# Gated linear attention and a maxout MoE: an earlier MoE 0 and 1, ScalarE's order in units 2 and 3, and a last output in column halves

## The chip, the cores and the metric

The kernel runs on one core of one Trainium2 chip. The metric is device time in microseconds, the median of several executions. A profiled execution also gives a trace of every engine. Its "span" runs from the first to the last instruction and is some 1.7 us shorter than the device time of the same run. TensorE is PE in the profile, VectorE DVE, ScalarE ACT, GpSimd POOL and SyncE, which issues nearly all transfers, SP.

## The reference

```python
state = zeros((B, H, D, D))                 # B, H, S, D = 4, 8, 768, 48
for t in range(S):
    state = alpha[:, :, t, :, None] * state + einsum('bhd,bhe->bhde', k[:, :, t], v[:, :, t])
    y[:, :, t] = einsum('bhd,bhde->bhe', q[:, :, t], state)
x = y.transpose(0, 2, 1, 3).reshape(B * S, H * D)     # 3072 x 384
g = maximum(x @ w1, x @ w2)                           # 384 x 1024 weights
return g @ w_out                                      # 1024 x 384
```

## The kernel before

The work is cut into 12 units of 256 tokens. Unit u goes through attention: a logarithm of alpha, prefix sums by products with masks, exponentials, scaled q and k, transposes ("turn"), scores and a running state. Then it goes through the MoE. Because max(h1, h2) = relu(h1 - h2) + h2, the hidden part is relu(x(w1 - w2)) and the output is that times wo, plus x(w2 wo). The product w2 wo is summed once, by `wmul`, and `wsub` makes w1 - w2. The MoE of unit u-1 runs inside the iteration of unit u, and units 0 and 1 are written out ahead of the loop. PSUM is the memory, in banks, that TensorE's products are written to; in this program a bank is used again once another engine has read the result out of it. A "hidden product" below is one call of `hid`, a group of six matmuls:

```python
def hid(u, f2, on_act=None):       # 6 products of 256 columns, then a Relu that frees one of two PSUM banks "m"
    ...
def outx(u, n): ...                # op = x * (w2 wo): 3 products of 384 columns
def outg(u, n): ...                # op += g * wo: 8 products, copy to SBUF, output DMA
def outp(u, n): outx(u, n); outg(u, n)

# ... ahead of the loop
wmul(0); wcast(1); wsub(0)
pmm(1, 1); pmask(1, 1)
wmul(1)
wout()
load(3)
hid(0, 0, True)
wsub(1)
hid(0, 1, True)
wsub(2)
dummies(2)                         # warm-up products, their result is never used
hid(0, 2, True)
wsub(3)
dummies(2)
vcast(1)
hid(0, 3, True)
load(4)
ln(2)
outp(0, 0)
...
for f2 in range(4):
    hid(1, f2)                     # MoE 1 ahead of the loop
ln(3)
load(5)
for u in range(2, NU):
    if u + 4 < NU: load(u + 4)
    kvmm(u, 0); pmm(u, 0); ...
    if u > 2: hid(u - 1, 0); hid(u - 1, 1); sumd(u + 1); hid(u - 1, 2)
    else:     outp(1, 0); sumd(u + 1)
    ...
outp(NU - 1, 0)
outp(NU - 1, 1)
```

A load of one unit is alpha, k, q, v, in this order, on SyncE's queue.

Names in the profile lines: af is alpha as loaded and lg its logarithm; cs the prefix sums and their exponentials; qn and kn the scaled q and k, tp and qk their turn; kv, tm and sb the running state; ya and xn the output of attention, xp and xt its turn ("x turn"); hp a hidden product and gT its Relu; op and outs an output; wq and w2o the product w2 wo; w the weights w1 - w2.

## Time and profile before

| | before |
|---|---|
| device time, median (range) | 148.25 us (148.0 to 148.4) |
| span of the profiled run | 147.0 us |
| hidden products of MoE 0, 1, 2 start at | 27.20, 39.55, 51.10 us |
| one unit of the loop | 9.58 to 9.77 us |
| last hidden products; end of the last product; end | 136.80; 143.60; 147.0 us |

The prediction reads the busy line and the chain. The stretch that the change rebuilds looks like this on PE's timeline (start, busy time, engine, line, operation, output from inputs, count, and in brackets the idle time before with its releaser):

```profile
25.24 2.12 PE L461 MATMUL wq<-wo,w2T 128*128 128x384 f16 x12
27.20 1.47 PE L410 MATMUL hp<-xt,w 128*128 128x256 f16 x12
28.70 0.59 PE L482 MATMUL warm<-wz 128*128 128x512 f16 x2
29.35 0.81 PE L410 MATMUL hp<-xt,w 128*128 128x256 f16 x6
...
39.55 2.97 PE L410 MATMUL hp<-xt,w 128*128 128x256 f16 x24 [0.61 <-DVE xt L399]
```

The second half of w2 wo comes first (25.24). Then warm-up products stand between the hidden products, and both use the two banks "m": the third hidden product starts at 29.35, just after the second Relu ends (29.30). Weights are not what the last two wait for: VectorE's last subtraction ends at 29.23, and the fourth product starts at 30.66. MoE 1 is a block of 24 matmuls by itself, behind an idle PE.

### The profile page before, as it was taken

What the parts mean: (1) busy time and instruction counts of PE and PEld (TensorE: products, weight loads), DVE (VectorE), ACT (ScalarE), POOL (GpSimd) and SP (SyncE); (2) the same over time, 40 slices, a digit from 0 to 9 for tenths busy, and PEclk for the clock granted to TensorE, in tenths of its full rate; (3) what the DMA queues carried; (4) which work ended last, traced back from release to release, by engine and by line L of the source; (5) the groups of instructions that cost most, each with busy time, mean ns of one, the idle gap of its engine ahead of it and who ended that gap; (6) DMA issues with size and microseconds to landing.
All of it is one profiled execution on the core that took longest, in us unless ns stands there. A gap on an engine that the chain in (4) does not pass through costs nothing.

```text
span 147.0 us, 4239 instructions
## 1 busy us (share of the span) xinstructions
PE 136.3 (93%) x1681; PEld 97.7 (66%) x1681; DVE 87.4 (59%) x180; ACT 97.2 (66%) x199; POOL 56.5 (38%) x111
## 2 busy tenths in 40 slices
PE   6749978999899999999999999999999999998990
PEld 2325655666776787767877877677777777775750
DVE  6046988904648876757767867566675756670010
ACT  3467452777576878688687886886879768654511
POOL 7491262055405438154181381541913617310000
PEclk9995999999999999999999999999999999999999
DMA  4999999969989897797999987999979991020202
GB/s 108 269 371 306 310 367 342 225 121 215 183 177 207 137 304 116 145 239 130 234 229 157 311 133 167 286 156 281 194 155 294 173 365 43 0 107 4 107 12 95
DMA packets 76339, 28.58 MB, mean 194 GB/s; under 512 B 71712, under 2 KB 74528, under 8 KB 76320
## 3 DMA queue, kind: packets, MB, share of 16 engines
q1 hardware_dynamic: 76320, 28.32, 83.4%
q8 instruction: 13, 0.21, 0.6%
q14 instruction: 6, 0.05, 0.1%
HBM read 23.59 MB, written 4.72 MB: 193 GB/s over the span
## 4 chain that ended last, share of the span: by engine, by line
PE 86%; ACT 4%; DVE 4%; DMA 3%; issue 1%
PE hp L410 23%; PE op L436 21%; PE op L429 8%; PE tp L296 7%; PE pp L345 5%; PE cs L237 4%; PE wq L461 3%; PE ya L381 3%; PE warm L482 3%; DMA af<-in_alpha_dram 3%; PE xp L397 3%; PE kv L318 2%; DVE qk L303 2%; PE cs L223 2%; PE ya L369 1%; ACT cs L252 1%
## 5 line engine op out<-in xcount | busy, mean ns | idle before, releaser
L410 PE MATMUL hp<-xt,w 128*128 128x256 f16 x288 | 37.2, 273 | 0.8 <-DVE xt L399 0.6
L415 ACT ACTIVATE gT<-hp 128x512 f16<-128x512 f32 x46 | 27.4, 596 | 14.4 <-PE hp L410 13.7
L351 DVE TENSOR_TENSOR pt<-pp,um 128x512 f16<-128x512 f32 x48 | 30.9, 686 | 9.3 <-PE pp L345 8.8
L436 PE MATMUL op<-wo,gT 128*128 128x384 f16 x192 | 35.1, 326 | 0.0
L285 POOL TENSOR_TENSOR kn<-kf,Em 128x384 f16<-128x384 f32 x24 | 23.4, 997 | 23.7 <-ACT Em L247 23.7
L410 PEld LDWEIGHTS <-w 128*128 128x128 f16 x288 | 26.1, 97 | 6.1 <-issue 2.2
L436 PEld LDWEIGHTS <-gT 128*128 128x128 f16 x192 | 18.4, 98 | 11.3
L277 POOL TENSOR_TENSOR sb<-tm,dd 128x192 f16<-128x192 f32 x20 | 10.1, 506 | 38.5 <-DVE tm L331 17.2
L439 ACT COPY outs<-op 128x384 f32<-128x384 f32 x24 | 11.5, 478 | 17.1 <-PE op L436 16.9
L289 DVE TENSOR_TENSOR qn<-qf,cs 128x384 f16<-128x384 f32 x24 | 12.3, 550 | 12.3 <-ACT de L257 11.6
L331 DVE TENSOR_TENSOR tm<-kv,sb 64x192 f32<-64x192 f32 x32 | 11.3, 353 | 9.1 <-PE kv L318 6.9
L429 PE MATMUL op<-w2o,xt 128*128 128x384 f16 x72 | 15.6, 326 | 0.0
L303 DVE COPY qk<-tp 128x1024 f16<-128x1024 f16 x20 | 12.9, 686 | 4.3 <-PE tp L296 4.3
L205 POOL CAST v<-vf 64x384 f16<-64x384 f32 x24 | 12.0, 501 | 6.4 <-DMA vf<-in_v_dram 5.6
L247 ACT ACTIVATE Em<-cs 128x384 f32<-128x384 f32 x24 | 11.6, 485 | 4.1 <-PE cs L237 4.1
L207 ACT CAST v<-vf 64x384 f16<-64x384 f32 x24 | 12.2, 510 | 1.4 <-DMA vf<-in_v_dram 0.9
L482 PE MATMUL warm<-wz 128*128 128x512 f16 x33 | 11.3, 452 | 1.3 <-DVE halves L149 1.3
L193 ACT ACTIVATE lg<-af 128x768 f16<-128x768 f32 x12 | 10.1, 843 | 3.2 <-DMA af<-in_alpha_dram 3.0
L252 ACT ACTIVATE cs<-cs 128x384 f32<-128x384 f32 x24 | 11.8, 493 | 0.0
L296 PE MATMUL tp<-ident,kn 128*128 128x128 f16 x96 | 9.3, 218 | 2.0 <-DVE qn L289 2.0
L345 PE MATMUL pp<-qk 48*128 48x128 f16 x192 | 9.8, 221 | 0.8 <-DVE qk L301 0.8
L388 ACT CAST xn<-ya 128x384 f16<-128x384 f32 x24 | 10.4, 491 | 0.1
(60 smaller groups left out, 152.7 us busy)
## 6 DMA issues: line engine op xcount, KB each, us to landing
af<-in_alpha_dram SPq DMA_DIRECT2D x12, 384.0 KB, 6.0
vf<-in_v_dram SPq DMA_DIRECT2D x12, 384.0 KB, 4.9
out_dram<-outs SPq DMA_DIRECT2D x11, 384.0 KB, 4.6
kf<-in_k_dram SPq DMA_DIRECT2D x40, 96.0 KB, 4.6
qf<-in_q_dram SPq DMA_DIRECT2D x40, 96.0 KB, 4.1
w2f<-in_moe_w_dram SPq DMA_DIRECT2D x3, 512.0 KB, 6.0
wof<-in_moe_w_out_dram SPq DMA_DIRECT2D x2, 768.0 KB, 7.6
w1f<-in_moe_w_dram SPq DMA_DIRECT2D x4, 384.0 KB, 9.6
```

Of the source, the lines that this page charges most:

```text
L252: nc.scalar.activation(out=X["csv"][cc], in_=X["csv"][cc], func=ACTF.Exp)
L285: nc.gpsimd.tensor_mul(out=X["kn"][cc][:, :, 0:D], in0=part(u, "kf", cc), in1=X["Em"][cc])
L289: nc.vector.tensor_mul(out=X["qn"][cc][:, :, 0:D], in0=part(u, "qf", cc), in1=X["csv"][cc])
L296: nc.tensor.transpose(tp[:, n, j, :], pair(src, j), ident)
L303: nc.vector.tensor_copy(out=X["qk"][:, cc], in_=tp.rearrange("p n h t -> p (n h) t"))
L345: nc.tensor.matmul(pa[a][:, j, :], lhsT=qk[r, 1, j, :], rhs=qk[r, 0, j, :], start=True, stop=True)
L351: nc.vector.tensor_mul(out=pt[:, a], in0=X["pa", cc][a], in1=um.unsqueeze(1).to_broadcast([128, HP, C]))
L410: nc.tensor.matmul(hp[:, n, :], lhsT=w12[:, ds, f * 128 : (f + 1) * 128], rhs=X["xt"][:, ds].rearrange("p n t -> p (n t)"), start=(ds == 0 ...
L415: nc.scalar.activation(out=gT[:, 2 * f2 : 2 * f2 + 2, :], in_=hp, func=ACTF.Relu)
L429: nc.tensor.matmul(op, lhsT=X["xt"][:, ds, n, :], rhs=w2o[:, ds, :], start=(ds == 0), stop=False)
L436: nc.tensor.matmul(op, lhsT=X["gT"][:, f, n * C : (n + 1) * C], rhs=wo16[:, f, :], start=False, stop=(f == NF - 1))
L482: nc.tensor.matmul(warm, lhsT=wz[:, 0:128], rhs=wz, start=True, stop=True)
```

## The change

The intent is to put the second half of w2 wo into the gaps between the hidden products of MoE 0, to take MoE 1 into the loop, to let ScalarE take the logarithm and the v casts of units 2 and 3 ahead of output copies, and to make the last copy and transfer half as large. The cut below leaves out some moves ahead of MoE 0 (`wcast(0)`, warm-up products and the second turn of unit 1), and that the sums of w2 wo move from the banks "m", which the hidden products between them now need, to g0 and g1.

```diff
 def turn(u, cc):
-    tp = new(f"g{cc}", ...)
+    tp = new(f"g{cc if u else 2 + cc}", ...)     # PSUM banks of unit 0's turns
...
+def outlast(u, n):
+    for e in range(2):                           # column halves of the last output
+        c = slice(e * DM // 2, (e + 1) * DM // 2)
+        op = new("m", [128, DM // 2], FP32, 2, "oq")
+        ...
+        if e == 0: scalar.copy(...);        scalar.dma_start(...)
+        else:      vector.tensor_copy(...); sync.dma_start(...)
...
-    pmm(1, 0)
-    pmask(1, 0)
     wmul(0)
     wcast(1)
     wsub(0)
-    pmm(1, 1)
-    pmask(1, 1)
-    wmul(1)
-    wout()
+    pmm(1, 0)
+    wmul(1, (0,))
     load(3)
     hid(0, 0, True)
     wsub(1)
+    wmul(1, (1,))
     hid(0, 1, True)
     wsub(2)
-    dummies(2)
+    wmul(1, (2,))
     hid(0, 2, True)
     wsub(3)
-    dummies(2)
+    pmask(1, 0)
+    wout()
+    dummies(1)
+    hid(0, 3, True)
     vcast(1)
-    hid(0, 3, True)
     load(4)
+    pmm(1, 1)
+    pmask(1, 1)
     ln(2)
     outp(0, 0)
...
-    outp(0, 1)
+    outx(0, 1)
+    outg(0, 1, (0, 1, 2, 3))
...
     vcast(2)
-    for f2 in range(4):
-        hid(1, f2)
+    outg(0, 1, (4, 5, 6, 7))
     ln(3)
...                                               # in the loop, every u, also u = 2:
+        hid(u - 1, 0)
+        hid(u - 1, 1)
...
-        xturn(u)
         if nxt:
+            xturn(u)
             vcast(u + 1)
-        if u + 2 < NU:
-            ln(u + 2)
-        if u > 2:
-            outg(u - 1, 1)
+            if u + 2 < NU:
+                ln(u + 2)
+            outg(u - 1, 1)
+        else:
+            outg(u - 1, 1, (0, 1, 2, 3))
+            xturn(u)
+            outg(u - 1, 1, (4, 5, 6, 7))
...
-    outp(NU - 1, 1)
+    outlast(NU - 1, 1)
```

More of the change, by code (lines that the diff above doesn't have):

```diff
@@ L292, in turn @@
         X = st[u]
-        tp = new(f"g{cc}", [128, 2, HP, C], FP16, 1, "tp")
+        tp = new(f"g{cc if u else 2 + cc}", [128, 2, HP, C], FP16, 1, "tp")
         for n, src in ((1, X["kn"][cc]), (0, X["qn"][cc])):
@@ L429, in outx, with outg @@
             nc.tensor.matmul(op, lhsT=X["xt"][:, ds, n, :], rhs=w2o[:, ds, :], start=(ds == 0), stop=False)
-    def outg(u, n):
+    def outg(u, n, fs=tuple(range(NF))):
         X = st[u]
-        d, b = divmod(u, B)
         op = X["op"]
-        for f in range(NF):
+        for f in fs:
             nc.tensor.matmul(
@@ L438, in outg, with dst @@
             )
-        nc.scalar.copy(out=X["outs"][:, n, :], in_=op)
-        t0 = b * S + d * 2 * C
-        dst = out[t0 : t0 + 2 * C, :].rearrange("(p j) d -> p j d", j=2)
-        if u == NU - 1:
-            nc.sync.dma_start(out=dst[:, n], in_=X["outs"][:, n])
-        elif n == 1:
-            nc.sync.dma_start(out=dst, in_=X["outs"])
+        if fs[-1] == NF - 1:
+            nc.scalar.copy(out=X["outs"][:, n, :], in_=op)
+            if u == NU - 1:
+                nc.sync.dma_start(out=dst(u)[:, n], in_=X["outs"][:, n])
+            elif n == 1:
+                nc.sync.dma_start(out=dst(u), in_=X["outs"])
+    def dst(u):
+        d, b = divmod(u, B)
+        t0 = b * S + d * 2 * C
+        return out[t0 : t0 + 2 * C, :].rearrange("(p j) d -> p j d", j=2)
+    def outlast(u, n):
+        X = st[u]
+        for e in range(2):
+            c = slice(e * DM // 2, (e + 1) * DM // 2)
+            op = new("m", [128, DM // 2], FP32, 2, "oq")
+            for ds in range(ND):
+                nc.tensor.matmul(op, lhsT=X["xt"][:, ds, n, :], rhs=w2o[:, ds, c], start=(ds == 0), stop=False)
+            for f in range(NF):
+                nc.tensor.matmul(
+                    op, lhsT=X["gT"][:, f, n * C : (n + 1) * C], rhs=wo16[:, f, c], start=False, stop=(f == NF - 1)
+                )
+            if e == 0:
+                nc.scalar.copy(out=X["outs"][:, n, c], in_=op)
+                nc.scalar.dma_start(out=dst(u)[:, n, c], in_=X["outs"][:, n, c])
+            else:
+                nc.vector.tensor_copy(out=X["outs"][:, n, c], in_=op)
+                nc.sync.dma_start(out=dst(u)[:, n, c], in_=X["outs"][:, n, c])
     def wturn(ds):
@@ L453, with wmul @@
     wqs = []
-    def wmul(n):
-        if n == 0:
-            wqs.extend([new("m", [128, DM], FP32, 2, "wq") for _ in range(2)] + [new("g3", [128, DM], FP32, 1, "wq")])
-        for ds in range(ND):
+    def wmul(n, dss=(0, 1, 2)):
+        if not wqs:
+            wqs.extend(new(f"g{i}", [128, DM], FP32, 1, "wq") for i in (0, 1, 3))
+        for ds in dss:
             for f in range(4 * n, 4 * n + 4):
@@ L529 @@
     xturn(0)
+    wcast(0)
+    dummies(2)
     turn(1, 0)
+    turn(1, 1)
     dummies(2)
-    turn(1, 1)
-    wcast(0)
-    pmm(1, 0)
-    pmask(1, 0)
     wmul(0)
@@ L573 @@
     turn(2, 1)
-    dummies(1)
     xturn(1)
-    dummies(1)
     vcast(2)
-    for f2 in range(4):
-        hid(1, f2)
+    outg(0, 1, (4, 5, 6, 7))
     ln(3)
@@ L594 @@
             kvmm(u, 1)
-        if u > 2:
-            hid(u - 1, 0)
-            hid(u - 1, 1)
-            if nxt:
-                sumd(u + 1)
-            hid(u - 1, 2)
-        else:
-            outp(1, 0)
+        hid(u - 1, 0)
+        hid(u - 1, 1)
+        if nxt:
             sumd(u + 1)
+        hid(u - 1, 2)
         if nxt:
@@ L613 @@
         pmask(u, 1)
-        if u > 2:
-            hid(u - 1, 3, True)
+        hid(u - 1, 3, True)
         if nxt:
@@ L622 @@
             state(u + 1, 0)
-        outp(u - 1, 0 if u > 2 else 1)
+        outp(u - 1, 0)
         yin(u)
@@ L627 @@
             turn(u + 1, 1)
-        if u > 2:
-            outx(u - 1, 1)
-        xturn(u)
+        outx(u - 1, 1)
         if nxt:
+            xturn(u)
             vcast(u + 1)
-        if u + 2 < NU:
-            ln(u + 2)
-        if u > 2:
+            if u + 2 < NU:
+                ln(u + 2)
             outg(u - 1, 1)
+        else:
+            outg(u - 1, 1, (0, 1, 2, 3))
+            xturn(u)
+            outg(u - 1, 1, (4, 5, 6, 7))
     for f2 in range(4):
```

## The prediction

> **What bounds the kernel now.** I first read the busy line and the slices of the page, to see where TensorE is not full.
>
> ```profile
> PE 136.3 (93%) x1681; PEld 97.7 (66%) x1681; DVE 87.4 (59%) x180; ACT 97.2 (66%) x199; POOL 56.5 (38%) x111
> ...
> PE   6749978999899999999999999999999999998990
> ...
> DMA  4999999969989897797999987999979991020202
> ```
>
> From about 40 to 133 us TensorE (PE) is full: windows of 10 us between 60 and 120 us have 10.00 us of PE busy. A unit of the loop takes 9.66 us (hidden products start at 51.10, and at 60.76 one unit later). A gain can only come from the first 43 us, from the end, or from work taken away. The DMA row says that the transfers are almost as full as PE.
>
> Next, the chain of work that ended last, from 20 us on:
>
> ```profile
> 20.86 0.43 PE warm L482 x2
> ...
> 21.77 0.70 DVE qk L301
> ...
> 28.70 0.61 PE warm L482 x2
> ...
> 37.75 1.29 DVE qk L303 x2
> 39.03 0.47 DVE xt L399
> ```
>
> Idle products ("warm") and waits on VectorE copies stand on the path. Adding the chain's useful PE pieces from 20.4 us (turn of unit 1) to 50.9 us (unit 3 enters the loop) gives 24.9 us (the largest: w2·wo 4.1, hidden products 5.2, output products 7.2) of 30.5, so 5.6 us are idle or warm-up: that is the most this stretch can give.
>
> Third, the timeline of the end:
>
> ```profile
> 134.23 0.87 ACT L388 CAST xn<-ya 128x384 f16<-128x384 f32 x2
> ...
> 135.16 0.51 PE L397 MATMUL xp<-ident,xn 128*128 128x128 f16 x6 [0.45 <-ACT xn L388]
> ...
> 135.50 1.46 PE L436 MATMUL op<-wo,gT 128*128 128x384 f16 x8
> 135.70 0.56 DVE L399 COPY xt<-xp 128x768 f16<-128x768 f16 x1 [3.31 <-PE xp L397]
> ...
> 143.64 0.48 ACT L439 COPY outs<-op 128x384 f32<-128x384 f32 x1 [1.31 <-PE op L436]
> ```
>
> PE waits for the xn casts with a ready product (outg of the unit before) behind them. After the last product the end is copy 0.48, DMA 1.85 (issue 144.15, landing 146.00) and closing 1.0 us.
>
> Last, whether the loads can follow an earlier PE. For each unit I set the landing of its loads against the instruction that uses them. Slack of alpha before its logarithm: unit 3 3.55, unit 4 2.56, unit 5 0.85, unit 6 1.47, unit 7 2.12 us, then 2 and more. The tightest use:
>
> ```profile
> 59.11 0.84 ACT L193 ACTIVATE lg<-af 128x768 f16<-128x768 f32 x1
> 60.19 0.48 ACT L439 COPY outs<-op 128x384 f32<-128x384 f32 x1 [0.24 <-PE op L436]
> ```
>
> Alpha of unit 5 was issued at 51.03 and took 7.23 us, so it landed at 58.26.
>
> **What the Trainium skill says.** "TensorE: Matmul & The Clock Gate", section "Wait — 56ns, not 53.3ns?": warm matmuls start every N/2.4 GHz plus about 2.5 ns; 384 columns give 162.5 ns, and the trace agrees (eight in 1.30 us). So 192 columns are estimated at 82.5 ns, and halving the columns of the last output costs PE nothing. "ScalarE: Activation LUTs", section "What ACT_TABLE_LOAD costs": an instruction with immediates takes 186 ns plus 0.833 ns an element; 384 give 506, measured 478. From these I estimate 0.32 us for 192. "DMA: Bandwidth & Descriptors", section "Specifications", wants at least 512 B for line rate; here 71712 of 76339 packets are smaller, which agrees with engines some 90% busy at a mean of 194 GB/s. The same page, "Issuing engines are not separate DMA queues": issuing from another engine saves only issue time, so the new ScalarE issue of the last output gets no bandwidth of its own; no run shows this yet.
>
> **The change, part by part.** The order of the built program keeps the source's order on each engine; the DMA queue's order is the same in both. Its waits are on earlier DMAs and on uses four units back, never on recent compute, so landings stay where they are. I replay the new order with durations from the trace.
>
> 1. Units 0 and 1, w2·wo, MoE 0. Before, from 27.36 to 31.47 the four hidden products take 4.11 us for 24 x 0.109 = 2.62. Now the second half of w2·wo (12 x 0.163) lies between them, while VectorE makes w1-w2. The w1 quarters land at 23.90, 25.03, 26.16, 27.34 and each subtraction takes 0.95, so they are ready at 24.9, 26.0, 27.15, 28.3. PE reaches the four hidden products at 25.0, 26.3, 27.6 and, behind one warm product and its drain (0.43), 28.7: none waits. The masks of unit 1 now follow the four subtractions (28.3 to 29.5), so its second score product waits 0.2; the three w2o copies on ScalarE end at 30.25 and hold the third output product 0.06. The output of MoE 0 ends at 31.75 instead of 33.19: gain 1.44.
> 2. Unit 2. ScalarE has v of unit 1 until 31.7 and the logarithm until 32.46 (before 33.21), so the sums gain only 0.75 at their start and 1.0 at their end, where the second output product gains 0.9. The exponentials end at 35.14, the first qn at 35.7; PE, with only half of that output product, arrives at 35.0 and waits 0.7. Turns end at 36.7, the x turn and the rest of the output product at 37.66. v of unit 2 lands at 37.21 and its casts hold the kv products to 37.8 and 38.34. The hidden products of MoE 1 start at 38.51 inside a normal iteration. Without stalls those of MoE 2 start 9.66 later, at 48.17; before 51.10. Gain 2.9.
> 3. In that iteration alpha of unit 3 (landing 38.97) makes the logarithm end at 39.85, so the first Relu is late and the third hidden product waits 0.4; q of unit 3 lands at 44.81, its second turn waits 0.2. MoE 2 starts at 48.8. Gain 2.3.
> 4. Alpha of unit 5 cannot land before 58.26. The logarithm then ends at 59.1 and the output copy behind it, in ScalarE's order, at 59.55. The second hidden product of MoE 3 needs that copy's bank and would be due at 59.1: it waits 0.45. Before it started at 61.42, now at 59.58. **Gain 1.84**, and everything afterwards keeps it: alpha of unit 6 is 0.4 late, inside the 0.9 that the copy has free; the rest has slack of 2 us.
> 5. The end. The half output product (0.65) now fills the wait for xn; but the x turn stays at 135.2 on the old clock, and the xt copy ends at 136.3, where the last hidden product starts instead of at 136.80: 0.46. The chain of Relus behind it makes 0.62 of it by the last output. The halves: the last matmul ends 0.6 earlier, VectorE's copy of 192 columns is 0.36 (estimate from 0.353 for tm, 192 columns) instead of 0.48, and the last DMA is half as large, which I count as 0.1, since 192 KB already take only 1.85. **Gain 0.9.**
>
> Removed: eight warm products in this stretch become five (three x 0.216), contained in the above. ScalarE's new order for units 2 and 3 removes no work. Sum: 1.84 + 0.9 = 2.7, and 148.12 - 2.7 = 145.4 us.
>
> **The rivals.** (a) *Loads do not bind*: then 2.3 + 0.9 = 3.2, 144.9 us. For it: the SP queue waits little for compute, and a shifted kernel could find its packets faster. Against it: the DMA row is at 9 in those slices and the issue chain of units 3 to 5 contains no wait on recent compute. (b) *The PE order costs more than replayed*: masks after all subtractions, w2o copies behind three Relus, MoE 1 inside the loop with ScalarE full. If the waits of parts 1 to 3 are 1 us more, gain falls to 1.3 + 0.9, 145.9 us. For it: ScalarE is in strict order and gets logarithms ahead of output copies; against: half a microsecond of such errors is hidden behind part 4. (c) *Fewer warm products let the clock fall*, as it did from 10 to 15 us (granted 0.66). A loss of 1 to 2 us, 146.5 us. Against: between 20 and 45 us my replay leaves no gap above 0.7 us, no larger than the gaps of before at 1.00. (d) *The end gives nothing*, because the last DMA has a fixed latency and closing is fixed: 0.6 instead of 0.9, 145.7 us.
>
> **Range and chances.** Part 4 makes the middle a minimum of two terms (about 2.3 and 1.84), so errors go mostly one way; a load landing 0.3 earlier or later moves it by that. I take 145.4 us, range 144.7 to 146.3. Faster by over 2% needs less than 145.16: 0.33. Within 2%: 0.65. Slower: 0.02.
>
> **What would show it.** In the new profile: MoE 0's hidden products starting without waits near 25, 26.3, 27.6 and 28.7; its first output product ending near 31.8; the hidden products of MoE 1 near 38.5; the logarithm of unit 5 directly behind its DMA near 58.3, with a hidden product held by the output copy behind it; the loop still 9.66 us a unit; the x turn of the last unit with no PE idle ahead of it, and landing to end of 1.0 us. The prediction is wrong if loads land at other times than before (then rival a), if PE waits over 0.5 us on masks, w2o or Relus in parts 1 to 3 (rival b), or if the granted clock falls below 1 after 20 us (rival c).

## More of the kernel before

Units 0 and 1 ("paired") get k and q in one transfer each with rows of 384 bytes. From unit 2 on, k and q come in four transfers each with rows of 192 bytes. The program has eight completion counters for transfers, used in turn (in the trace of before, 130 transfers finish on eight semaphores, 16 or 17 on each), so a load can also have to wait for the transfer eight earlier.

## The result and the profile after

| | before | after |
|---|---|---|
| device time, median (range) | 148.25 us (148.0 to 148.4) | 146.32 us (145.31 to 146.52) |
| ratio, with 95% interval | | 0.9856 [0.9815, 0.9897] |
| span of the profiled run | 147.0 us | 143.6 us |
| hidden products of MoE 0, 1, 2, 3 | 27.20, 39.55, 51.10, 60.76 | 25.07, 38.75, 48.41, 58.08 |
| last hidden products; end of the last product; end | 136.80; 143.60; 147.0 | 133.66; 140.48; 143.6 |

A ratio is the mean time of one kernel's fast runs over that of the other's of the same rounds, so it is not quite the ratio of the medians. Executions over 1.5% slower than the fastest of the same kernel are left out of the means. The change is 1.4% faster by it, which at a threshold of 2% is "the same". Note that the profiled run of after was its fastest (145.31), and that of before (148.74) slower than the timed ones. So the two traces differ by 3.4 us where the medians differ by 1.9. That spread of the changed kernel became the main question.

The page of after, the lines that answer to those in the prediction (busy time and its share, then tenths in 40 slices):

```profile
PE 134.4 (94%) x1689; PEld 97.1 (68%) x1689; DVE 87.4 (61%) x180; ACT 97.1 (68%) x200; POOL 56.6 (39%) x111
...
PE   6868879998999999999999999999999999999991
...
DMA  3999999978999999997998989999999785020203
```

PE is busy 1.9 us less, although it has eight more products (the halved columns add eleven, and three warm-up products go), and its share rose by a point because the span fell more. From 10 to 15 us the granted clock was 1.00, where the profile of before had 0.64 to 0.68. Fuller than before are the second, third and seventh slice (7, 4 and 8 tenths there) and those of the end. PE's timeline of after shows the new MoE 0 and 1:

```profile
24.05 0.82 PE L483 MATMUL wq<-wo,w2T 128*128 128x384 f16 x4
25.07 0.83 PE L410 MATMUL hp<-xt,w 128*128 128x256 f16 x6 [0.19 <-DVE w L498]
25.73 0.81 PE L483 MATMUL wq<-wo,w2T 128*128 128x384 f16 x4
...
28.78 0.82 PE L410 MATMUL hp<-xt,w 128*128 128x256 f16 x6
...
38.75 1.47 PE L410 MATMUL hp<-xt,w 128*128 128x256 f16 x12
```

The w2 wo products now lie between the hidden products, and none of these waits but the first, 0.19 us for its w1 - w2. MoE 1 starts at 38.75 inside a loop iteration (12 matmuls in a row, as in every later unit), and that iteration takes 48.41 - 38.75 = 9.66 us, as the next one (9.67). The end, on the timeline of all engines:

```profile
131.55 0.87 ACT L388 CAST xn<-ya 128x384 f16<-128x384 f32 x2
...
131.86 0.81 PE L435 MATMUL op<-wo,gT 128*128 128x384 f16 x4
...
132.51 0.50 PE L397 MATMUL xp<-ident,xn 128*128 128x128 f16 x6
...
132.84 0.81 PE L435 MATMUL op<-wo,gT 128*128 128x384 f16 x4
...
133.66 3.03 PE L410 MATMUL hp<-xt,w 128*128 128x256 f16 x24
...
140.52 0.36 DVE L466 COPY outs<-oq 128x192 f32<-128x192 f32 x1 [3.10 <-PE oq L459]
140.90 0.33 SPq L467 DMA_DIRECT2D out_dram<-outs  x1
```

The x turn (132.51) has no idle PE ahead of it, since half of an output product (four matmuls from 131.86) fills the time; before it had 0.45 us. The last copy is 0.36 us, and its transfer lands at 142.51, 1.61 us after the start of its issue (before 1.85 for twice the bytes).

Finally, the wait that the prediction made its pin, the logarithm of unit 5, on ScalarE's timeline of after:

```profile
56.42 0.84 ACT L193 ACTIVATE lg<-af 128x768 f16<-128x768 f32 x1
57.50 0.48 ACT L439 COPY outs<-op 128x384 f32<-128x384 f32 x1 [0.24 <-PE op L435]
```

Alpha of unit 5 was issued at 50.58 and landed at 56.18 here. In before those were 51.03 and 58.26. The copy at 57.50 waits only for its product, and no hidden product waits for it. So the wait that was to hold the gain at 1.84 us does not occur.

### The profile page after: what moved, and what is told of

Its sections match the earlier page's. It is cut to its first block, busy times and chain, and to the rows that moved or that the text cites. A ratio compares the mean times of both kernels' runs of the same rounds, so it can differ in the third digit from the quotient of the medians.

```text
span 143.6 us, 4259 instructions
## 1 busy us (share of the span) xinstructions
PE 134.4 (94%) x1689; PEld 97.1 (68%) x1689; DVE 87.4 (61%) x180; ACT 97.1 (68%) x200; POOL 56.6 (39%) x111
## 4 chain that ended last, share of the span: by engine, by line
PE 76%; SPq 10%; DMA 6%; ACT 3%; DVE 1%; issue 1%; ACTq 0%
PE hp L410 23%; PE op L435 20%; PE op L429 8%; SPq L75 6%; PE tp L296 6%; DMA w1f<-in_moe_w_dram 6%; PE pp L345 4%; PE ya L381 3%; PE cs L237 3%; PE xp L397 3%; PE kv L318 2%; SPq L115 2%; SPq L121 1%; PE ya L369 1%; PE cs L223 1%; ACT gT L415 1%
## 5 line engine op out<-in xcount | busy, mean ns | idle before, releaser
L415 ACT ACTIVATE gT<-hp 128x512 f16<-128x512 f32 x47 | 28.1, 597 | 16.2 <-PE hp L410 15.5
L435 PE MATMUL op<-wo,gT 128*128 128x384 f16 x184 | 34.0, 326 | 0.0
L435 PEld LDWEIGHTS <-gT 128*128 128x128 f16 x184 | 17.5, 98 | 10.5
L439 ACT COPY outs<-op 128x384 f32<-128x384 f32 x23 | 11.0, 477 | 13.7 <-PE op L435 13.7
L429 PE MATMUL op<-w2o,xt 128*128 128x384 f16 x69 | 15.0, 326 | 0.0
L504 PE MATMUL warm<-wz 128*128 128x512 f16 x30 | 10.0, 447 | 1.3 <-DVE halves L149 1.3
```

What stands on the lines that cost most here:

```text
L415: nc.scalar.activation(out=gT[:, 2 * f2 : 2 * f2 + 2, :], in_=hp, func=ACTF.Relu)
L429: nc.tensor.matmul(op, lhsT=X["xt"][:, ds, n, :], rhs=w2o[:, ds, :], start=(ds == 0), stop=False)
L435: nc.tensor.matmul(op, lhsT=X["gT"][:, f, n * C : (n + 1) * C], rhs=wo16[:, f, :], start=False, stop=(f == NF - 1))
```

## The experiments

Each was timed against before on the same chip: chip 11 for experiments 1 to 8, chip 2 for 9 to 11, chip 8 for 12. Before took 147.9 to 148.65 us throughout, on each of the three. Edits are to the changed kernel unless said.

My theory at the start was that something in the loads of units 3 to 5 binds in some runs and not in others. The rival was that the order on the engines costs the difference.

**1. The changed kernel again.** No edit.

> The changed kernel itself, unchanged, for a second profile and more times. Its profiled run gave 145.31 us and the other four 146.0 to 146.5, all at a granted clock of 1.00. Theory L (the loads pace the kernel at units 3 to 5): the time follows the landing of alpha of unit 5, which was at 56.18 us in the fast profile; a run of about 146.3 should show it about 1 us later (57 to 57.5), with the logarithm of unit 5 starting within 0.3 us of the landing. Rival P (TensorE's own order costs more than I replayed, and the landing is not involved): the landing stays near 56.2 and PE waits appear elsewhere between 20 and 45 us.

Measured: 145.69 us (145.42 to 146.74), ratio 0.9831 [0.9787, 0.9875]. By luck this profile caught the slow end: 146.74 us, span 145.0, clock 1.0. Its critical chain (start, us, what) in the iteration of MoE 1:

```profile
33.97 6.34 DMA af<-in_alpha_dram
40.30 0.02 issue
40.33 0.84 ACT lg L193
41.17 0.50 ACT gT L415
...
41.71 0.82 PE hp L410 x6
```

Alpha of unit 3 lands at 40.30. The logarithm follows, then the first Relu of MoE 1 behind it in ScalarE's order, and the third hidden product (41.71) needs the bank that this Relu frees. In the fast profile alpha landed at 38.63, and the same logarithm and third product are

```profile
38.66 0.84 ACT L193 ACTIVATE lg<-af 128x768 f16<-128x768 f32 x1
...
40.27 0.81 PE L410 MATMUL hp<-xt,w 128*128 128x256 f16 x6
```

Of the 1.67 us by which alpha is later, 0.78 are a later issue (33.97 against 33.19) and the rest a longer transfer. The iteration took 10.90 us in place of 9.66, so the slow profile loses 1.24 of the 1.4 us between the two spans there. Alpha of unit 5 landed at 57.46, where theory L had it, and again held nothing: its logarithm came 0.40 later, behind the v casts. Its issue to landing took 5.33 us, where before had 7.23.

**2. Alpha one unit ahead of k, q and v, from unit 4 on.**

```diff
-        load_a(u)
+        if u < 4: load_a(u)
+        if 3 <= u < NU - 1: load_a(u + 1)
```

> The changed kernel with the alpha of units 4 and on loaded one unit earlier in the queue (ahead of k, q, v of the unit before); same bytes, same packets. Theory L: alpha of units 4 and 5 lands well before its logarithm (slack over 1 us instead of 0.1 to 0.3), and since k, q and v of these units had 1.8 to 3 us of slack the kernel gets 0.3 to 1 us faster than the changed kernel, 145.3 to 145.9 us. Rival P: within 0.2 us of the changed kernel.

Measured: 146.91 us (146.49 to 147.48), ratio 0.9903 [0.9861, 0.9945], so slower than the changed kernel beside it (0.9831; the two intervals just overlap). Theory L had it faster. Alpha of unit 4 went ahead (41.00), but k and q of unit 3 fell behind it. The last q of unit 3 landed at 46.00, and PE's second turn waited:

```profile
46.70 0.38 PE L299 MATMUL tp<-ident,kn 128*128 128x128 f16 x4 [1.43 <-DVE qn L292]
```

In this stretch loads have no slack to give each other: what one gains another loses.

**3. Light loads.** k and q of units 2 and later in rows of 1536 bytes at the same number of transfers, with wrong data.

```diff
-   in_=rows(src, u, cc * C, C).rearrange("h (p j) d -> j p h d", j=2)[j],
+   in_=<one contiguous piece of the same size>.rearrange("(p h d) -> p h d", p=64, h=H),
```

> The changed kernel with k and q of units 2 and on read as rows of 1536 B from other places of the same tensors instead of 192 B: same bytes, same number of transfers, an eighth of the packets. Wrong result on purpose. Theory L: loads land earlier from unit 2 on, no logarithm waits for its landing, and the kernel is 0.5 to 1.5 us faster than the changed kernel, 144.7 to 145.6 us, with less spread between runs. Rival P: within 0.3 us of the changed kernel, about 146.2.

Measured: 145.41 us (145.21 to 145.94), ratio 0.9804 [0.9772, 0.9837]; in its profile the iteration of MoE 1 took 9.66 us. That is 0.3 us below the median of the run beside it. The two intervals overlap, so the times alone show no cost of the loads, and the gain and the narrower spread that theory L expected did not clearly come.

**4. The same light loads in before.**

> The kernel before with the same light loads (wrong result on purpose). Theory L says that in the kernel before the loads had slack everywhere (0.85 us at the tightest), so it stays within 0.3 us of 148.2. If it gets faster by more than 0.5 us, the loads bound the kernel before too, and slack read from landings is not the whole of it.

Measured: 148.07 us (147.94 to 148.12), ratio 0.9977 [0.9951, 1.0002]. At most 0.5% there: before was not bound by loads. That the earlier PE brings one of them onto the path is read from the profiles of experiments 1 and 9.

**5. Before with only the new banks of unit 0's turns.** My prediction had passed over this line of the diff.

```diff
-        tp = new(f"g{cc}", ...)
+        tp = new(f"g{cc if u else 2 + cc}", ...)
```

> The kernel before with one line of the change: the first two turns take banks 2 and 3 in place of 0 and 1, so they need not wait for the exponentials that read banks 0 and 1. Theory N (the start gives nothing that lasts): the turns of unit 0 come about 0.7 us earlier and the x turn of unit 0 near 18.9 in place of 19.88, but the first hidden product of MoE 0 only near 26.6 to 27.2, because the second half of the w2 wo sum and its casts stand ahead of it, and the time is 147.9 to 148.4, ratio 0.995 to 1.000. Rival S (the missed line is a large part of the gain): everything after the x turn moves by the same 1 us, first hidden product at 26.2, time near 147.2, ratio 0.992 or less.

Measured: 147.84 us (147.61 to 148.36), ratio 0.9972 [0.9935, 1.001]. In its profile the x turn of unit 0 came at 18.70 (before 19.88) and the first hidden product at 26.09 (before 27.20). The positions are those of rival S and the time is that of theory N. The profiled run of before had a low clock (0.64 to 0.68 from 10 to 15 us; 0.988 as a mean over the run). Of the 24 runs of before in these experiments two had a mean of 0.988 and the others 0.997 or more, so the comparison of profiles overstates the gain. A gain of up to 0.7%, not separated from zero.

**6. The changed kernel with the old banks.**

> The changed kernel with the first turns back in banks 0 and 1. Theory N (the landing of w1, not the start, sets MoE 0): x turn of unit 0 later by up to 1 us, but the w1 quarters land at 24.0 to 27.5 as before and the hidden products of MoE 0 start at 25.1, 26.4, 27.7, 28.8 or within 0.3 of that; the time equals the changed kernel's, ratio 0.980 to 0.988. Rival S: the first hidden product moves to 26 and the time is about 1 us longer, ratio near 0.991.

Measured: 146.84 us (145.45 to 147.59), ratio 0.9912 [0.9872, 0.9952]. The profile shows what theory N said: the x turn 0.33 later at 19.17, but the hidden product of MoE 0 at 24.85, set by the landing of w1, and a span of 143.7. But the ratio is rival S's number: the profiled run was the fastest, and the three timed ones took 146.76 to 147.59. They left no trace, and the interval overlaps that of the changed kernel, so whether the banks matter in those runs stays open.

**7. The changed kernel with the whole old end.**

```diff
-            xturn(u)                    # last unit: between the halves of the product
+        xturn(u)                        # ahead of the whole product
-    outlast(NU - 1, 1)
+    outp(NU - 1, 1)
```

> The changed kernel with the whole old end: last output in one piece, x turn of the last unit ahead of the whole product of the unit before. The prediction gave the end 0.9 us; the two traces show 0.72 to 0.76 from the first hidden product of MoE 3 to the end. Expected: 86.2 us from that product to the end as in the kernel before (changed kernel 85.5), and 0.75 us longer than the changed kernel, ratio 0.986 to 0.993. If the end gives nothing (rival d was 0.6 in place of 0.9), the stretch is 85.6 and the ratio that of the changed kernel, 0.983.

Measured: 146.71 us (146.05 to 147.25), ratio 0.9885 [0.9837, 0.9932]. From the first hidden product of MoE 3 to the end of the span it took 144.5 - 58.24 = 86.26 us, against 85.52 in the changed kernel and 86.24 in before. The new end is worth 0.74 us. The positions divide it: 0.46 us up to the last hidden products, nothing from there to the end of the last product (6.80 us in this kernel and 6.82 in the changed one), and 0.3 us in the last copy and transfer.

**8. q of unit 2 issued by ScalarE**, in a pause near 24 us (from 22.96 in its profile), so that SyncE gets to alpha of unit 3 earlier.

```diff
     wcast(1)
+    for cc in range(2): load_rows(2, "qf", q, cc, nc.scalar)   # no longer in load(2)
```

> The changed kernel with the four q loads of unit 2 issued by ScalarE, idle near 24 us, in place of SyncE, whose issues run without a pause from 24.7 to 36 us (0.65 to 0.9 us each). Theory Q (what varies in the iteration of MoE 1 is when SyncE gets to issue alpha of unit 3, behind eight loads of unit 2): alpha of unit 3 is issued some 2.5 to 3 us earlier and lands by 37, its logarithm never waits, that iteration takes 9.66 to 9.76 us in the profile, all runs are near 145.2 to 145.4, ratio 0.979 to 0.981. Rival B (bandwidth, not issue: the earlier packets only slow the others): w1 quarters or v of unit 2 land later by 0.3 or more, alpha of unit 3 at 38 or later, time as the changed kernel's or longer, ratio 0.983 to 0.990. Sign that would refute both: the Relus of MoE 0 late because ScalarE issues.

Measured: 146.41 us (146.29 to 146.7), ratio 0.9869 [0.9842, 0.9896]. Rival B's numbers came, but its reason is not the only one. SyncE's waits (waited for: us in total, times, longest) have new lines, the longest

```profile
SPq L75 <- DMA w1f<-in_moe_w_dram: 4.0, 1, 4.0
```

The eight completion counters are used in turn by all transfers, whichever engine issues them. The four new transfers moved the turn, so that alpha of unit 2 had to wait at SyncE for a w1 quarter. It was issued at 25.21 in place of 20.82 and landed at 33.23 in place of 31.10, and MoE 1 started 1.4 us later (40.15). The wait does not explain all of it. In the changed kernel the issue of this alpha itself took 3.83 us, here 0.37, so it ended only 0.93 us later (25.58 against 24.65). The other 1.2 us came after the issue, with q's transfers (issued from 22.96 to 25.71) now ahead of it or beside it, which is what rival B said. The run doesn't separate the two further. No issue time was gained: SyncE issued alpha of unit 3 at 33.54, in the changed kernel at 33.19.

**9. Alpha of unit 3 later, on purpose**: behind four of its own k and q loads.

```diff
             load_kq(u, 0)
+            if u == 3: load_a(u)        # and not ahead of load_kq(3, 0)
             load_kq(u, 1)
```

> The changed kernel with alpha of unit 3 issued behind the first four k and q loads of unit 3 in place of ahead of them. Theory A (one wait varies: the logarithm of unit 3 waits for alpha, and the iteration of MoE 1 is 9.66 us plus the time by which alpha lands later than 0.11 us after the first hidden product of MoE 1; four profiles so far fit this within 0.02: landing minus product -0.12, 0.36, 0.49, 1.35 us, iteration 9.66, 9.91, 10.04, 10.90): alpha lands 1.5 to 3 us later than in them, at 41 to 42.5, and the iteration is 9.66 plus (landing - product - 0.11) again, some 12 to 13.3 us; later iterations stay at 9.66 to 9.76; the time is 147.3 to 148.9, ratio 0.992 to 1.003. Rival B (landing times only go along with something else, or other queues of work hide it): the iteration stays under 11 us and the time under 146.8.

Measured: 147.68 us median of the three fast runs (147.44 to 147.93), ratio 0.996 [0.9933, 0.9987], so 1.4 us over the changed kernel's 146.32 and within what theory A gave. The profiled run was slow, at 151.31 us with clock 0.974. What happened up to the clock's fall is still readable on PE's timeline:

```profile
38.72 1.47 PE L413 MATMUL hp<-xt,w 128*128 128x256 f16 x12
42.83 0.37 PE L226 MATMUL cs<-halves,lg 128*128 128x4 f16 x8 [2.64 <-ACT lg L196]
43.31 1.44 PE L413 MATMUL hp<-xt,w 128*128 128x256 f16 x6
```

Alpha landed at 41.91. Without a wait the third hidden product starts 1.52 us after the first; here it started 4.59 after, a wait of 3.07. Theory A had it at 41.91 - 38.72 - 0.11 = 3.08. Then came what I had not expected. The six products took 1.44 us where they take 0.81, and the table by stretches (busy time of each engine, then granted clock, DMA share and GB/s) shows why:

```profile
40.00:42.50 2.50, 0.19 (x2) 0.00 (x0) 0.97 (x3) 0.57 (x1) 0.00 (x0) 1.00 0.98 162
42.50:45.00 2.50, 2.07 (x18) 1.18 (x20) 0.00 (x0) 1.46 (x4) 0.00 (x0) 0.56 0.91 226
```

PE did nothing for 2.64 us (40.19 to 42.83). The clock was granted at 1.00 up to 42.8 and at 0.50 from there to 49.6 us. The iteration took 15.70 us: 9.66, the wait of 3.07, and a remainder of 2.97, put down to the clock. My expected 12 to 13.3 us for the iteration missed by that last term.

**10. Alpha of unit 3 ahead of v of unit 2.**

```diff
+        if u == 2: load_a(3)
         load_v(u)
```

> The changed kernel with alpha of unit 3 issued ahead of v of unit 2. Theory A: alpha lands about 0.6 us earlier, 38 to 39.7, so up to 0.6 of the wait in the iteration of MoE 1 goes; v of unit 2 lands 0.6 to 1 later, near 38, and its casts hold the first hidden product of MoE 1 by 0 to 0.7 (its slack was 0.02 us ahead of the cast, and some 0.3 from the cast to the kv product). Sum between 0.3 faster and 0.3 slower than the changed kernel, ratio 0.981 to 0.987. If v is not tight (rival V), 145.5 us, ratio 0.979 to 0.981.

Measured: two fast runs, 146.93 and 147.33 us, ratio 0.9923 [0.9889, 0.9956], and two slow ones at lower clock (149.94 and 151.38). Alpha of unit 3 landed at 37.01, and the iteration of MoE 1 had no wait (9.67 us). But v of unit 2 landed at 38.97, and its casts held PE:

```profile
39.57 0.33 PE L321 MATMUL kv<-v,kn 128*128 128x96 f16 x4 [1.49 <-POOL v L208]
```

MoE 1 started at 40.34. The expectation had the exchange of one wait for the other and not its size: v came some 2.2 us later than in the changed kernel (36.78), not 0.6 to 1.

**11. Unit 2 paired**: its k and q in one transfer each, with rows of 384 bytes.

```diff
-    PAIRED = (0, 1)
+    PAIRED = (0, 1, 2)
```

> The changed kernel with unit 2 treated as units 0 and 1 are: its k and q come in one load each with rows of 384 bytes in place of four loads with rows of 192, at the cost of eight more kv products on TensorE (16 take 0.70 us, 8 some 0.45) and two more casts on GpSimd. Theory A with a limit by small rows: alpha of unit 3 is issued some 5 us earlier and lands by 37, the iteration of MoE 1 is 9.66 to 9.76, the first hidden product of MoE 1 is 0.25 to 0.4 later than 38.75 for the products added: 145.5 to 145.9 in all runs, ratio 0.980 to 0.984, little spread. Rival B (the bytes, not the rows, set the landings, as in the run with q of unit 2 on ScalarE): alpha of unit 2 lands later than 32 and alpha of unit 3 not before 38.5; 146.3 to 147.2, ratio 0.985 to 0.991.

Measured: 145.56 us (145.49 to 145.69), ratio 0.982 [0.9796, 0.9843]. SyncE now issues alpha of unit 3 at 30.23 (start, us, first lines of unit 2's v and unit 3's alpha):

```profile
28.66 1.52 SPq L75 DMA_DIRECT2D vf<-in_v_dram  x1
30.23 1.42 SPq L75 DMA_DIRECT2D af<-in_alpha_dram  x1
```

In the changed kernel the same two were

```profile
32.52 0.63 SPq L75 DMA_DIRECT2D vf<-in_v_dram  x1
33.19 0.58 SPq L75 DMA_DIRECT2D af<-in_alpha_dram  x1
```

Alpha landed at 36.66, the iteration of MoE 1 took 9.67 us, and MoE 1 started at 38.97, 0.22 later for the kv products added. All four runs are within 0.2 us, as theory A said. Experiment 3 had longer rows in the old number of transfers, and there this alpha was issued at 32.88 and landed at 38.14. So the earlier issue came with the smaller number of transfers, two in place of eight for k and q, and not with the longer rows.

**12. Experiment 11 with the logarithm of unit 2 ahead of the v casts of unit 1**, and its sums ahead of unit 1's kv products: an attempt at more.

```diff
+    ln(2)
     vcast(1)
...
-    ln(2)
     outp(0, 0)
+    sums(2)
     kvmm(1, 0)
...
-    sums(2)
```

> A version meant to beat both: unit 2 paired as in the run before, and the logarithm of unit 2 ahead of ScalarE's casts of v of unit 1, with its sums ahead of the kv products of unit 1 on TensorE. In the profile of the paired run alpha of unit 2 lands at 30.27, but its logarithm starts at 31.81 behind two casts (1.03 us), and TensorE then waits 0.16 us for the sums and 0.49 us for q of unit 2. If alpha of unit 2 is the limit there: logarithm at 30.75, sums at 31.8 right behind the output product, exponentials 0.6 earlier, no wait for q, first hidden product of MoE 1 near 38.4 in place of 38.97, time near 145.0, ratio 0.977 to 0.980. If the casts of v, now 0.85 later, take the place of the wait (kv products of unit 1 and the state behind them, then xn): first hidden product at 38.9 to 39.3 and 145.5 to 146, ratio 0.981 to 0.985.

Measured: 145.72 us (145.55 to 145.74), ratio 0.9821 [0.98, 0.9842]. The sums did move to 31.70, but the wait changed its name, as the second alternative said:

```profile
35.47 0.27 PE L369 MATMUL ya<-sb,qk 48*128 48x48 f16 x8 [0.89 <-DVE tm L331]
```

The state of unit 1 now comes last (PE waits 0.89 us for it), and MoE 1 starts at 39.09. No gain.

## Why the prediction was right and where it was wrong

Seven profiles put the cause in one table. "Late" is the landing of alpha of unit 3 minus the start of MoE 1's first hidden product, and the wait is how much later than 1.52 us after it the third hidden product starts.

| run | MoE 1 starts | alpha of unit 3 | late | wait of the third product | iteration |
|---|---|---|---|---|---|
| 11, unit 2 paired | 38.97 | 36.66 | -2.31 | 0.00 | 9.67 |
| after, first profile | 38.75 | 38.63 | -0.12 | 0.00 | 9.66 |
| 7, old end | 38.67 | 39.03 | 0.36 | 0.24 | 9.91 |
| 2, alpha ahead | 38.49 | 38.90 | 0.41 | 0.29 | 11.55 (also q of unit 3) |
| 6, old banks | 38.52 | 39.01 | 0.49 | 0.37 | 10.04 |
| 1, after again | 38.95 | 40.30 | 1.35 | 1.24 | 10.90 |
| 9, alpha late | 38.72 | 41.91 | 3.19 | 3.07 | 15.70 (also clock) |

Where alpha is late the wait is the lateness less 0.11 us, within 0.01 in each run; where it is early there is none. The other four profiles of changed kernels fit: alpha lands 0.52 us (3), 0.1 us (8), 3.33 us (10) and 2.52 us (12) ahead of the product, and the product does not wait. Moving alpha by hand, in runs 9 and 11, moves the wait as this says.

**What was right.** The class and the mechanism of parts 1 to 3. MoE 0's hidden products started at 25.07, 26.38, 27.69 and 28.78 (predicted 25.0, 26.3, 27.6, 28.7), and MoE 1 at 38.49 to 38.95 in the profiles that leave unit 2's loads as they are (predicted 38.51). In the fast profile MoE 2 started at 48.41, a gain of 2.69 over before (predicted 2.9 without stalls). Part 3's first wait is real: with alpha at 38.97, as assumed, the rule above gives 0.35 us (predicted 0.4). The granted clock stayed at 1.00 after 20 us in the changed kernel, so rival (c) did not come. The estimates for half as many columns held too: the last products of 192 columns start 0.083 us apart (three in 0.25 us from 139.41; predicted 82.5 ns), and ScalarE's copy of 192 columns takes 0.32 us.

**What failed: part 4, "Alpha of unit 5 cannot land before 58.26."** It rested on "so landings stay where they are". They did not. Alpha of unit 5 landed at 56.18 and 57.46 in the two profiles of the changed kernel, because issue to landing took 5.60 and 5.33 us in place of 7.23 (issued at 50.58 and 52.13, in before at 51.03). Its logarithm held no hidden product in either. The prediction had named this itself as a sign of being wrong, "if loads land at other times than before". The 1.84 us of part 4 was no ceiling. The gain of the middle is part 2 less the wait of part 3, and that wait is a draw. So the gain came to 2.68 us in the fast profile and 1.24 in the slow one, read at the start of MoE 3 (58.08 and 59.52 against 60.76). I had treated one measured landing as a fixed time, and so chose the later pin.

**Part 5 was mis-sized.** 0.9 us was predicted (its terms 0.62, 0.12 and 0.1 add to 0.84) and 0.74 measured. The step "the chain of Relus behind it makes 0.62 of it by the last output" gave nothing beyond 0.46, because the 24 hidden products and the Relus take the same time in both ends (6.80 and 6.82 us to the last product). The smaller copy and transfer gave 0.3 in place of 0.22 (0.12 + 0.1).

**The sum.** Middle and end make 2.68 + 0.74 = 3.4 us in the fast profile, which is 147.0 - 143.6, and 1.24 + 0.74 = 2.0 in the slow one, which is 147.0 - 145.0. Both are counted from the profiled run of before (148.74 us, with its low clock). From the 148.12 us that the prediction started from, the changed kernel's extremes of 145.31 and 146.74 are 2.8 and 1.4 us faster. The prediction's 2.7, and its 145.4 us, lie between. That they lie so close to the best run is luck: the pin that set 1.84 never acted, the wait that did act varies from run to run, and the end was put 0.16 too high. The median of the first call, 146.32, is 0.02 above the range, that of the second, 145.69, inside it. Rival (a), "loads do not bind" with 144.9 us, describes the best runs but not their size; in the slow profile a load does bind, that of unit 3, which part 3 had given 0.4 us, and not that of unit 5. Rival (b), 145.9 us, is nearest to the mean of the timed runs (146.00), but its sign, waits of over 0.5 us on masks, w2o or Relus, did not come in the fast profile: the longest wait between 24 and 41 us is 0.54 us for qn (predicted 0.7). In the slow profile the third product does wait for a Relu, behind a logarithm that waits for its load. Whether another order on ScalarE would shorten this was not tested. It could not remove it, since PE's own sums need that logarithm and wait 0.80 us for it just ahead (41.22).

**What stays open.** Why the same load takes 5.44 us in one run and 6.34 in another, and which waits the unprofiled runs had, above all in experiment 6, whose slowest run (147.59 us) is 2.1 us over its profiled one. The light loads of experiment 3 still spread by 0.7 us.

**A better version.** Runs 11 and 12 together have nine times within 145.49 to 145.74 us, where the changed kernel's nine runs lie between 145.31 and 146.74, at a mean of 146.00. Pairing unit 2 takes the draw out of the time at 0.2 us of PE work. The intervals of the ratios still overlap, so a lower mean is likely and not proven, while the smaller spread is plain in these runs. They were on chips 2 and 8 and the changed kernel's second call on chip 11, but before spread alike on all three.

## What to carry to other kernels

When a change pulls the compute earlier against a full load queue, list for each load its landing against its first use, and treat every landing as a range taken from several runs, not as a time. The tightest early use will then decide from run to run, and what helped here was to issue that load earlier by making those ahead of it fewer and larger, while reordering loads that had no slack (experiments 2 and 10) only moved the wait. A new issuer or a new order of transfers also moves which counter each waits for, so read the queue's own waits after any such edit.

## What the Trainium skill lacked or had wrong

- "TensorE: Matmul & The Clock Gate", section "HAM oscillation — how this bites in real kernels", warns of PE-idle gaps longer than some 3.4 us. In the profile of experiment 9 the granted clock fell to 0.50 at the end of a gap of 2.64 us, and stayed there until 49.6 us; that iteration lost 2.97 us beyond the wait. In the profile of before it fell to 0.50 from 10.9 to 14.3 us, where the longest PE gap ahead of it was 1.20 us (7.62 to 8.82). So a shorter gap than that can go with a fall. That the gap caused it was not tested, and three other runs of experiment 9, whose gaps no trace shows, kept 1.00.
- "DMA: Bandwidth & Descriptors", section "Issuing engines are not separate DMA queues", says that a second issuer only saves issue time. In experiment 8 it saved none and the kernel lost some: through the program's shared completion counters SyncE waited 4.0 us for a w1 quarter, and alpha of unit 2 landed 2.1 us later (33.23 against 31.10), in part for that reason.
- No page gives a spread for one transfer in a full queue. The same alpha of unit 5 took 7.23, 5.60 and 5.33 us from issue to landing in three profiles, and alpha of unit 3 took 5.44 and 6.34 us in two profiles of one kernel.
